# A fused attention and snake-MLP kernel: weights and values loaded in 128-partition parts, value passes by even and odd dimensions, stage orders written anew

## The chip, the cores and the metric

The kernel runs on one core of a Trainium2 chip. The metric is device time in microseconds (us), the median of several executions. Inside the core, five engines work from their own in-order queues and meet only at semaphores: TensorE (PE in the profile, its weight loads PEld), VectorE (DVE), ScalarE (ACT), GpSimd (POOL) and SyncE (SP). SP only issues transfers here; POOL issues transfers too, between its multiplications, and those are the only ones that convert float32 to bfloat16 on the way. All transfers are carried by the core's 16 DMA engines.

## What is computed

```python
def rmsnorm(x, g):
    rms = np.sqrt(np.mean(x * x, axis=-1, keepdims=True) + 1e-06)
    return x / rms * g
q_n, k_n = (rmsnorm(q, g_q), rmsnorm(k, g_k))          # 8 batches, 12 heads, 448 rows, 64 dims
scores = scale * np.matmul(q_n, k_n.transpose(0, 1, 3, 2))
attn = softmax(scores)
x = np.matmul(attn, v)                                  # then heads are joined: 3584 rows x 768
h = x @ w_in                                            # 768 x 2048
g = h + sin(alpha * h) ** 2 / (alpha + 1e-09)
out = g @ w_out                                         # 2048 x 768
```

All inputs and the output are float32.

## The kernel before

**Stages.** One stage is one batch `b` of eight. In a stage the 12 heads are taken as three chunks of four heads (`c` = 0, 1, 2; four heads are two `pp` times two `hi`). A chunk is loaded by `load_qk` (L149, buffers for three chunks), squared (token `q`, L256 on POOL or L253 on ACT), reduced (`u`, L262), turned into 1/rms (`r`, L271 and L272), the q half multiplied by both gains (`g`, L259), scaled to bfloat16 (`k`, L281), and transposed to head dimension by row: either by the DMA (`t`, L291) or by TensorE through PSUM (`p`, L304). Chunk numbers in tokens count from the stage's own batch: 0, 1, 2 are its own chunks, 3, 4, 5 the next batch's, 6 and 7 only occur in loads (`l`).

**Attention part of a stage.** `scores` (token `S`, 21 a stage: 7 key tiles for each of three chunks) runs four 64x64 matmuls (L326) and one exponential on ACT (L329). `attend` (L335) sums over keys: `o` and `v` for chunk 0 (sums of the exponentials, then values), `x` for the sums of chunks 1 and 2 together, `y` and `z` for their values. With chunks 1 and 2 a value pass handles half of the 64 dimensions, so that eight 32-column tiles fill the array: `y` takes dimensions 0 to 31, `z` 32 to 63. L364 divides and writes `xT`, the input of the MLP, with one 128-row block `kt` for each of six slices of the 768 rows. Which 32-row strip a head gets within a block is told by `strip` (L144). The rows of `w_in` have to lie in the same order, and `load_w_in` (L209) does that: two transfers of 128 partitions for chunk 0, two for chunk 1, and four of 32 partitions for chunk 2, for each half of the 2048 columns.

**The two products.** `first_product` (L384) runs 96 matmuls of 128x128 by 448 columns (L392), then the snake: sine on ACT (L370), square on POOL for even `m` (L373) and on ACT for odd `m` (L375), and L378 on DVE. `second_product` of batch `b` (L422) is cut into small steps of eight matmuls (L471) which the next stage's order puts between its scores: a digit in an order is that many steps of the current unit, `f` one of the unit after. The last batch has it at the end, whole-array (L452).

**What sets the order.** Nothing is scheduled by the compiler. `STAGE_0`, `STAGE_1` and `STAGE_N` (L32 to L58; `STAGE_N` serves batches 2 to 7) each hold a list of tokens, a list of the four PSUM bank pairs in the order in which they are taken (`bank_pair`, L132), and tasks to be done at given steps of `first_product` (key -1 to 8). Each token puts its instructions on their engines' queues in that order, so a token that waits holds up what stands behind it on the same engine. `V` loads the values of a coming batch, `W` a half of `w_in`, `O` a half of `w_out`, all from POOL; `D` is a small copy with which POOL waits for an earlier load before it issues further ones. The transfers that POOL issues share eight completion semaphores in turn, so POOL doesn't issue one before the transfer eight places earlier has landed. `blank` matmuls (L234, L322) only keep TensorE busy in the first stage.

Of the kernel before, what the change touches and what calls it, by code (L numbers as in the profile page):

```python
# [17 lines left out]
try:  # L18
# [6 lines left out]
BF16 = mybir.dt.bfloat16  # L25
# [5 lines left out]

STAGE_0 = (  # L32
    (
        "q01 L q00 u01 G u00 g0 r01 k01 q10 r00 b11 u10 q11 k00 b15 g1 u11 q20 D1 l3 p011 r1 V0 p00 u20 "
        "q21 S4 k11 S g2 S2 S3 S1 S2 k10 l4 u21 W0 r2 p1 k20 S1 S2 S1 S q31 k21 S1 D2 o1 u31 o1 q30 S2 o5 "
        "p2 S1 S1 q41 u30 v4 S q40 v3 u41 u40 W1 S S S O0 S1 S2 S y5 x7 y2 z7 r3 g3 O1 l5 r4 V1 "
    ),
    "232013331201201032132103203103210231022301230123",
    {-1: 'g4 k30 k31', 0: 'l6', 1: 'k410 k400', 2: 'k401', 3: 'D4 k411', 4: 't4', 5: 'p3 l7 q50', 6: 'q51 u50', 7: 'g5', 8: 'u51'},
)  # L40
STAGE_1 = (
    (
        "2 f f 1 f 1 S f 3 S 1 q30 S r2 2 k20 k21 1 t2 S 1 S 4 S S 2 q40 2 S o3 o2 S o1 S u30 f f l5 f o1 "
        "u40 1 f f q31 1 q41 1 u31 S 1 u41 S 3 S r3 2 g3 f f S f r4 f 1 S g4 1 k30 S V1 2 k41 2 S k40 k31 "
        "q50 v2 S g5 v5 S S t3 x4 S z5 x3 q51 y7 z2 u51 "
    ),
    "0123230231301231202021213201230132103210",
    {-1: 'l6', 0: 'l7', 2: 't4', 4: 'u50'},
)
STAGE_N = (  # L50
    (
        "r2 S 1 q40 5 f f f k20 f 1 S 3 f 1 f u40 S S f 1 k21 1 q41 q31 1 t2 S 1 V1 1 S 1 g4 1 S 2 u31 S "
        "1 u41 S 2 S f f 1 S 2 S 2 q30 S 1 S o6 o1 v4 1 v1 u30 S v1 g3 r4 v1 f f 1 k41 2 S 1 S 1 l5 1 f "
        "q50 S f k40 f S f 1 q51 t4 S 1 r3 1 k30 1 k31 S 1 x1 l6 x6 y4 y1 y2 z2 z2 z2 z1 "
    ),
    "32103020210230230310310132131313103210210",
    {-1: 'g5 t3', 0: 'u50', 5: 'u51', 6: 'l7'},
)  # L58
LAST = "0123012"

# [7 lines left out]
def kernel(  # L68
# [23 lines left out]
    nc = tc.nc  # L92
    B, H, S, D = q.shape
    D_MODEL = H * D
    D_FF = moe_w_in.shape[1]
    P = 128
    KT = D_MODEL // P
    MT = D_FF // P
    NP = H // 2
    NT = S // P  # L100
    REST = S - NT * P
    NJ = S // REST
    assert P == 2 * REST == 2 * D
    NC = NP // 2
    SCALE = float(D) ** -0.5
    HALF = D_MODEL // 2
# [7 lines left out]
    vpool = ctx.enter_context(tc.tile_pool(name="vpool", bufs=2))  # L114
# [17 lines left out]
    def bank_pair(name, dtype=F32):  # L132
        slot = int(upcoming.popleft())
        free_at.remove(slot)
        ps = psum.tile([P, 2, 2048 // mybir.dt.size(dtype)], dtype, tag=f"ps{slot}", name=name)
        slot_of[id(ps)] = slot
        return ps

    def give_back(ps):
        free_at.append(slot_of.pop(id(ps)))  # L140

    qk, vb, norm = {}, {}, {}

    def strip(c, pp, hi):  # L144

        s = 2 * hi + (pp if c == 1 else 1 - pp)
        return slice(s * 32, s * 32 + 32)

    def load_qk(ci, k_queue=nc.sync):  # L149

        b, dp = ci // NC, ci % NC
        qk[ci] = inp.tile([P, 2, 2 * NJ, D], F32, tag="qk", name="qk")
        for which, src, queue in ((0, q, nc.sync), (1, k, k_queue)):
            heads = src[b].rearrange("(dp hi pp) (p j) d -> dp (pp p) hi (j d)", hi=2, pp=2, j=NJ)[dp]
            queue.dma_start(out=qk[ci][:, which].rearrange("p (hi j) d -> p hi (j d)", hi=2), in_=heads)

    def load_v(b):


        vb[b] = vpool.tile([P, NP, NJ, D], BF16, tag="vb", name="vb")  # L160
        heads = v[b].rearrange("(g pp) (p j) d -> (pp p) g (j d)", pp=2, j=NJ)
        nc.gpsimd.dma_start(out=vb[b].rearrange("p g j d -> p g (j d)"), in_=heads)

    load_qk(0, nc.scalar)
    small = const.tile([MT, P], F32)
# [9 lines left out]
    ones = const.tile([P, D], BF16)  # L175
# [11 lines left out]
    w_in_sb = [wpool.tile([P, KT, D_FF // 2], BF16, name=f"w_in_{half}") for half in range(2)]  # L187
    w_out_sb = wpool.tile([P, MT, D_MODEL], BF16)
# [17 lines left out]
        give_back(ps)  # L206
        nc.vector.reciprocal(inv_alpha_sb, alpha_sb)

    def load_w_in(half):  # L209


        cols = slice(half * D_FF // 2, (half + 1) * D_FF // 2)
        pairs = moe_w_in.rearrange("(c hi pp d) f -> c pp hi d f", c=NC, pp=2, d=D)
        quarters = moe_w_in.rearrange("(g x d) f -> g x d f", x=2, d=D // 2)
        for pp in range(2):
            nc.gpsimd.dma_start(out=w_in_sb[half][:, pp], in_=pairs[0, pp, :, :, cols])
        for x in range(2):
            nc.gpsimd.dma_start(out=w_in_sb[half][:, 2 + x], in_=quarters[4:8, x, :, cols])
        for hi in range(2):
            for pp in range(2):  # L220
                g = 8 + 2 * hi + pp
                nc.gpsimd.dma_start(out=w_in_sb[half][strip(2, pp, hi), 4:6], in_=quarters[g, :, :, cols].rearrange("x d f -> d x f"))

    def load_w_out(half):
        src = moe_w_out.rearrange("(mt p) d -> p mt d", p=P)
        cols = slice(half * HALF, (half + 1) * HALF)
        nc.gpsimd.dma_start(out=w_out_sb[:, :, cols], in_=src[:, :, cols])  # L227

    def keep_busy(n, rhs):


        ps = bank_pair("ps")
        for _ in range(n):
            nc.tensor.matmul(ps[:, 0, :rhs.shape[-1]], blank[:, :P], rhs, start=True, stop=True)  # L234
        give_back(ps)
# [99 lines left out]
    def attend(b, what, tiles=range(NJ)):  # L335

        kind, both = what.split()
        both = both == "1"  # L340
        if tiles[0] == 0:
            avs[what] = bank_pair("av")
        av = avs[what]
        for j in tiles:
            for hi in range(2):
                for c in ((1, 2) if both else (0,)):
                    for pp in range(2):
                        r = slice(pp * 64, pp * 64 + 64)
                        o, k = (strip(c, pp, hi), c - 1) if both else (slice(hi * 64, hi * 64 + 64), pp)
                        d = slice(D // 2) if kind in ("ones", "low") and both else slice(D // 2, D) if both else slice(D)  # L350
                        w = ones[r, d] if kind == "ones" else vb[b][r, 2 * c + hi, j, d]
                        nc.tensor.matmul(av[o, k, :S], w, expT[b * NC + c, j][r, hi, :], start=(j == 0), stop=(j == NJ - 1))  # L352
        if tiles[-1] < NJ - 1:
            return
        if kind == "ones":
            rec = recs[both] = rpool.tile([P, 2, S], F32, tag="rec", name="rec")
            nc.scalar.activation(rec, av[:, :, :S], ACT.Ln)
            nc.scalar.activation(rec, rec, ACT.Exp, scale=-1.0)
            give_back(avs.pop(what))
        else:  # L360
            if b not in xT:
                xT[b] = xpool.tile([P, KT, S], BF16, tag="xT", name="xT")
            kts = slice(0, 2) if not both else slice(2, KT, 2) if kind == "low" else slice(3, KT, 2)
            nc.vector.tensor_mul(xT[b][:, kts, :], av[:, :, :S], recs[both])  # L364
            give_back(avs.pop(what))
# [135 lines left out]
    def step(b, token):  # L501

        what, n = token[0], [int(x) for x in token[1:]]
        if what == "b":
            keep_busy(int(token[1:]), blank)
        elif what == "G":
            spread_g()
        elif what == "L":
            spread_alpha()
        elif what == "W":  # L510
            load_w_in(n[0])
        elif what == "O":
            load_w_out(n[0])
        elif what == "V":
            if b + n[0] < B:
                load_v(b + n[0])
        else:
            ci = NC * b + n[0]
            if ci >= NC * B:
                return  # L520
            if what == "l":
                return load_qk(ci)
            if ci not in norm:
                norm[ci] = norm_tasks(ci)
            st = norm[ci]
            if what == "D":
                nc.gpsimd.tensor_copy(gate, qk[ci][:, 1, 0, 0:1])
            elif what == "q":
                st.square(n[1])
            elif what == "u":  # L530
                st.reduce(n[1])
            elif what == "g":
                st.fold_g()
            elif what == "r":
                st.rsqrt(slice(n[1], n[1] + 1) if n[1:] else slice(0, 2))
            elif what == "k":
                st.scale(n[1], n[2:] or (0, 1))
            elif what == "p":
                st.pe_transpose((0, 1), n[1:2] or (0, 1), act=len(n) > 2)
            elif what == "t":  # L540
                st.transpose()
            else:
                raise ValueError(token)

    UNIT = MT // 2
    for b in range(B):
# [7 lines left out]
        for x in tokens_of(plan):  # L554
# [4 lines left out]
            elif x[0] in STEPS:  # L559
                n = int(x[1:] or 1)  # L560
# [38 lines left out]
```

## Time and profile before

| | us |
|---|---|
| Device time, median of 3 | 463.21 (461.94 to 466.78) |
| Span of the profiled execution | 463.5 |
| PE busy | 413.9 (89%) |
| ACT busy | 316.3 (68%) |
| POOL busy | 275.1 (59%) |
| DVE busy | 225.8 (49%) |

Read from the start of the 96 matmuls of `first_product` in each batch, the stages lie like this (us from the start of the span):

| batch | attention part | first product |
|---|---|---|
| 0 | 0 to 37.7 | 37.7 to 72.2 |
| 1 | 72.2 to 107.4 | 107.4 to 126.5 |
| 2 | 126.5 to 162.5 | 162.5 to 180.7 |
| 3 | 180.7 to 214.4 | 214.4 to 232.7 |
| 4 | 232.7 to 264.1 | 264.1 to 282.4 |
| 5 | 282.4 to 316.9 | 316.9 to 335.2 |
| 6 | 335.2 to 367.7 | 367.7 to 386.0 |
| 7 | 386.0 to 415.7 | 415.7 to 434.0 |
| second product of batch 7 | 434.0 to 463.5 | |

A line of the waits reads: engine, line and tile that waited, what it waited for, then the total in us, the number of waits and the longest. A line of the timeline reads: start, length, engine, line, operation, tile written and read, count, and in brackets the idle time before it with what ended it. In the windows the columns after the length are the busy times of PE, PEld, DVE, ACT and POOL with instruction counts, the granted TensorE clock (1.00 is full), the busy share of the 16 DMA engines, and the rate at which bytes landed.

### The profile page before, as it was taken

The page shows a single profiled execution, that of the slowest core. Times are in us where ns is not written, and L with a number is a line of the kernel's source. Part 1 is how long each engine was busy: PE and PEld are TensorE (multiplying, and loading weights), DVE is VectorE, ACT ScalarE, POOL GpSimd, SP SyncE. Part 2 cuts the span into 40 slices and gives each one's busy share as a digit, 9 for nine tenths or more (in the row PEclk, how much of TensorE's full clock was granted, in tenths as well). Part 3 has the DMA queues.
Part 4 walks back from the last instruction along what each step waited for, and adds up shares of the span by engine and source line. Part 5 has one row for each costly group of instructions (what it writes and reads, how often), then busy time and mean ns, then how long its engine had stood idle before and what let it go on. Part 6 is the DMA issues. An engine that isn't in the chain of part 4 may idle for free.

```text
span 463.5 us, 14846 instructions
## 1 busy us (share of the span) xinstructions
PE 413.9 (89%) x6598; PEld 245.6 (53%) x6598; DVE 225.8 (49%) x331; ACT 316.3 (68%) x465; POOL 275.1 (59%) x251
## 2 busy tenths in 40 slices
PE   4988099878996999979998999979997999999796
PEld 2444046643573655655565556655574656655363
DVE  4743157433762356723765356524764365344411
ACT  4796068882896668956888778956896778976400
POOL 5945497895494945956486946856495945003200
PEclk9999689998998899989999999989999999999899
DMA  6998899799029490567419570949329510620013
GB/s 238 187 213 104 112 238 179 146 213 239 4 56 180 62 245 3 98 153 152 140 28 222 101 193 3 114 136 184 108 57 196 103 33 1 110 55 0 2 46 90
DMA packets 73188, 54.99 MB, mean 119 GB/s; under 512 B 44564, under 2 KB 68900, under 8 KB 73124
## 3 DMA queue, kind: packets, MB, share of 16 engines
q1 hardware_dynamic: 54834, 40.51, 38.6%
q0 software_dynamic: 17344, 11.83, 19.0%
q10 hardware_dynamic: 946, 1.70, 1.0%
q8 instruction: 51, 0.84, 0.8%
q14 instruction: 13, 0.11, 0.1%
HBM read 45.62 MB, written 11.01 MB: 122 GB/s over the span
## 4 chain that ended last, share of the span: by engine, by line
PE 71%; DMA 21%; POOL 3%; issue 2%; ACT 2%; DVE 1%; POOLq 0%; SPq 0%; ACTq 0%
PE hps L392 28%; PE ops L471 21%; DMA qkT<-qkn 14%; PE av L352 8%; PE sc L326 6%; PE ops L452 5%; DMA w_in<-in_moe_w_in_dram 3%; DMA qk<-in_k_dram 3%; PE ps L234 2%; DMA small<-in_moe_alpha_dram 1%; POOL qk L259 1%; POOL sq L256 1%; ACT s L370 1%; ACT expT L329 1%; POOL w_out_sb L227 1%
## 5 line engine op out<-in xcount | busy, mean ns | idle before, releaser
L329 ACT ACTIVATE expT<-sc 128x896 bf16<-128x896 f32 x168 | 142.9, 917 | 34.8 <-PE sc L326 34.4
L392 PE MATMUL hps<-xT,w_in 128*128 128x448 bf16 x768 | 149.8, 356 | 13.1 <-DVE qkn L281 12.1
L471 PE MATMUL ops<-w_out_sb,g_sb 64*64 64x384 bf16 x3072 | 154.6, 329 | 0.5 <-issue 0.5
L392 PEld LDWEIGHTS <-w_in 128*128 128x128 bf16 x768 | 74.9, 99 | 87.4 <-DVE qkn L281 12.6
L471 PEld LDWEIGHTS <-g_sb 64*64 64x64 bf16 x3072 | 99.7, 109 | 38.4 <-issue 2.1
L373 POOL TENSOR_TENSOR s<-s 128x448 f32<-128x448 f32 x64 | 59.6, 932 | 99.6 <-ACT s L370 68.3
L370 ACT ACTIVATE s<-hps,alpha_sb 128x448 f32<-128x448 f32 x128 | 74.0, 626 | 62.4 <-PE hps L392 47.2
L378 DVE SCALAR_TENSOR_TENSOR g_sb<-s,inv_alpha_sb,hps 128x448 bf16<-128x448 f32 x128 | 81.5, 677 | 63.4 <-POOL s L373 62.2
L281 POOL TENSOR_TENSOR qkn<-qk,inv 128x448 bf16<-128x448 f32 x80 | 72.8, 938 | 37.2 <-ACT inv L272 31.4
L326 PE MATMUL sc<-qkT 64*64 64x448 bf16 x672 | 68.5, 356 | 17.8 <-DMA qkT<-qkn 15.9
L256 POOL TENSOR_TENSOR sq<-qk 128x896 f32<-128x896 f32 x44 | 73.6, 1681 | 6.5 <-DMA qk<-in_k_dram 6.4
L262 DVE TENSOR_REDUCE ms<-sq 128x14 f32<-128x896 f32 x44 | 47.1, 1081 | 16.4 <-POOL sq L256 16.3
L364 DVE TENSOR_TENSOR xT<-av,rec 128x896 bf16<-128x896 f32 x24 | 25.6, 1089 | 57.0 <-PE av L352 38.9
L477 DVE COPY osb<-ops 128x384 f32<-128x384 f32 x48 | 26.7, 557 | 50.7 <-PE ops L471 50.7
L259 POOL TENSOR_TENSOR qk<-qk,gg 128x896 f32<-128x896 f32 x24 | 50.1, 2089 | 2.1 <-ACT gg L198 1.5
L352 PE MATMUL av<-expT,vb 64*32 64x448 bf16 (+1 forms) x1120 | 41.8, 358 | 4.6 <-issue 4.6
L326 PEld LDWEIGHTS <-qkT 64*64 64x64 bf16 x672 | 24.9, 107 | 34.7 <-DMA qkT<-qkn 18.3
L375 ACT ACTIVATE s<-s 128x448 f32<-128x448 f32 x64 | 36.9, 577 | 3.1 <-DVE g_sb L378 0.8
L352 PEld LDWEIGHTS <-vb 64*32 64x32 bf16 (+1 forms) x1120 | 21.1, 97 | 16.5 <-issue 7.2
L478 DVE TENSOR_TENSOR osb<-osb,ops 128x384 f32<-128x384 f32 x48 | 26.6, 554 | 1.7
L352 PE MATMUL av<-expT,ones 64*32 64x448 bf16 (+1 forms) x672 | 25.3, 350 | 0.0
L452 PE MATMUL ops<-w_out_sb,g_sb 128*128 128x384 bf16 x128 | 22.4, 341 | 3.1 <-DVE g_sb L378 3.1
(48 smaller groups left out, 167.4 us busy)
## 6 DMA issues: line engine op xcount, KB each, us to landing
qk<-in_q_dram SPq DMA_DIRECT2D x24, 448.0 KB, 5.6
qk<-in_k_dram SPq DMA_DIRECT2D x22, 448.0 KB, 6.1
out_dram<-osb SPq DMA_DIRECT2D x39, 192.0 KB, 3.0
vb<-in_v_dram POOLq DMA_DIRECT2D x8, 672.0 KB, 9.8
w_out_sb<-in_moe_w_out_dram POOLq DMA_DIRECT2D x2, 1536.0 KB, 20.1
out_dram<-osb SPq DMA_DIRECT2D x26, 96.0 KB, 3.0
w_in<-in_moe_w_in_dram POOLq DMA_DIRECT2D x8, 256.0 KB, 16.7
w_in<-in_moe_w_in_dram POOLq DMA_DIRECT2D x8, 128.0 KB, 16.6
```

Source lines behind the costliest of these rows:

```text
L256: nc.gpsimd.tensor_mul(st.sq[w], qk[ci][:, w], qk[ci][:, w])
L259: eng.tensor_mul(qk[ci][:, 0], qk[ci][:, 0], gg.to_broadcast([P, 2 * NJ, D]))
L262: nc.vector.reduce_sum(st.ms[:, w, :], st.sq[w], axis=AX.X)
L281: eng.tensor_mul(n[:, :, hi, :], x[:, hi], inv[:, hi].unsqueeze(2).to_broadcast([P, NJ, D]))
L326: nc.tensor.matmul(sc[pp * 64:pp * 64 + 64, hi, :S], qkt[r, 1, j * REST:(j + 1) * REST], qkt[r, 0, :], start=True, stop=True)
L329: nc.scalar.activation(expT[c, j], sc[:, :, :S], ACT.Exp, scale=SCALE)
L352: nc.tensor.matmul(av[o, k, :S], w, expT[b * NC + c, j][r, hi, :], start=(j == 0), stop=(j == NJ - 1))
L370: nc.scalar.activation(s1, hps, ACT.Sin, scale=alpha_sb[:, m, :])
L373: nc.gpsimd.tensor_mul(s2, s1, s1)
L378: nc.vector.scalar_tensor_tensor(g_sb[:, m, (b % 2) * S:(b % 2 + 1) * S], s2, inv_alpha_sb[:, m, :], hps, op0=ALU.mult, op1=ALU.add)
L392: nc.tensor.matmul(ps[:, m % 2, :S], w_in_sb[m * 2 // MT][:, kt, m % (MT // 2) * P:(m % (MT // 2) + 1) * P], x[:, kt, :], start=(kt == ORD ...
L471: nc.tensor.matmul(st["ps"][os, r, :HALF], g_sb[rs, m, c0 + o * 64:c0 + o * 64 + 64], w_out_sb[rs, m, half * HALF:(half + 1) * HALF], star ...
```

## The change

- `w_in` comes in by half and chunk (`load_w_in(half, c)`). For chunks 1 and 2 one transfer brings 256 rows to 128 partitions, partition `p` taking rows `2p` and `2p + 1`. No 32-partition transfers are left: four transfers a half in place of eight.
- That puts even rows into one block and odd rows into the next, so the value passes `y` and `z` take the even and the odd dimensions, with weights read at a step of two.
- In chunk 2 the two heads of a pair sit the other way round in the strips. So that the strips are right, chunk 2's q, k and v are loaded with the two 64-partition halves exchanged: two transfers of 64 partitions in place of one of 128.
- `v` comes by chunk (`load_v(b, c)`: one, one and two transfers, in place of one for all), and each half of `w_out` in two parts.
- All three orders, bank lists and task lists are new. Batch 1's third chunk is squared already in the first stage, and batch 1's second and third chunks are transposed by TensorE (56 more transposing matmuls, 36 DMA transposes in place of 40), and in `STAGE_N` the loads of `v` stand ahead of the scaling of chunk 2 and in the first product, no longer right behind its transposes.

The transfers are meant to use the DMA engines better and to bring what is needed first, and the orders are meant to fit them.

```diff
@@ STAGE_N (tokens; tasks beside the first product) @@
-        "r2 S 1 q40 5 f f f k20 f 1 S 3 f 1 f u40 S S f 1 k21 1 q41 q31 1 t2 S 1 V1 1 S 1 g4 1 S 2 u31 S "
-        "1 u41 S 2 S f f 1 S 2 S 2 q30 S 1 S o6 o1 v4 1 v1 u30 S v1 g3 r4 v1 f f 1 k41 2 S 1 S 1 l5 1 f "
-        "q50 S f k40 f S f 1 q51 t4 S 1 r3 1 k30 1 k31 S 1 x1 l6 x6 y4 y1 y2 z2 z2 z2 z1 "
+        "1 r2 q31 q30 f 2 S V10 f 3 V11 f f 2 S k20 3 S 2 k21 S u31 q40 1 t2 2 S 1 f u30 g3 S 2 f S f S "
+        "r3 q41 f f 1 l5 1 f S 3 u40 1 S S 5 S S u41 o7 v7 S S 5 S 2 q51 k31 f S 2 S q50 k30 2 S g4 1 u50 "
+        "S 2 r4 t3 1 S z3 x7 k40 y7 z1 z2 z1 "
...
-    {-1: 'g5 t3', 0: 'u50', 5: 'u51', 6: 'l7'},
+    {-1: 'l6 u51 V12', 1: 'k41', 2: 't4 l7', 3: 'g5'},
@@ STAGE_0 (tokens from the first W on; tasks) @@
-        "... W0 r2 p1 k20 S1 S2 S1 S q31 k21 S1 D2 o1 u31 o1 q30 S2 o5 "
-        "p2 S1 S1 q41 u30 v4 S q40 v3 u41 u40 W1 S S S O0 S1 S2 S y5 x7 y2 z7 r3 g3 O1 l5 r4 V1 "
+        "... V00 q11 u11 p00 q10 V02 W11 p011 S4 u10 q20 r1 "
+        "g1 S4 q21 S1 l3 u20 S1 k11 k10 S4 u21 S g2 r2 p1 k20 S2 V01 S2 S o3 q30 W00 S W12 k21 l4 o4 D2 "
+        "q40 W01 p2 l5 S1 g4 S u30 q31 W02 g3 u40 v1 q41 S v6 u31 S W10 S S3 S1 S3 x2 S S x1 S1 u41 x2 y2 "
+        "q51 y3 x2 z1 z1 y2 z1 z1 q50 r4 r3 z2 z1 O00 k31 "
...
+    {-1: 'u50 k30 u51 O01', 1: 'k401 O10', 2: 'k410 k411', 3: 'O11', 4: 'V10', 5: 'k400', 6: 'D4 l6 V11', 7: 'p3', 8: 'V12 g5 l7 p4'},
@@ load_qk @@
+            if dp < 2:
+                queue.dma_start(out=rows, in_=heads.rearrange("pp p hi x -> (pp p) hi x"))
+            else:
+                for pp in range(2):
+                    queue.dma_start(out=rows[pp * 64:pp * 64 + 64], in_=heads[1 - pp])
@@ load_w_in(half, c) @@
-        for x in range(2):
-            nc.gpsimd.dma_start(out=w_in_sb[half][:, 2 + x], in_=quarters[4:8, x, :, cols])
-        for hi in range(2):
-            for pp in range(2):
-                g = 8 + 2 * hi + pp
-                nc.gpsimd.dma_start(out=w_in_sb[half][strip(2, pp, hi), 4:6], in_=quarters[g, :, :, cols].rearrange("x d f -> d x f"))
+        rows = moe_w_in[c * 2 * P:(c + 1) * 2 * P, cols]
+        if c:
+            nc.gpsimd.dma_start(out=w_in_sb[half][:, 2 * c:2 * c + 2], in_=rows.rearrange("(p x) f -> p x f", x=2))
@@ attend @@
-                        d = slice(D // 2) if kind in ("ones", "low") and both else slice(D // 2, D) if both else slice(D)
+                        d = slice(kind == "high", D, 2) if both and kind != "ones" else slice(D // 2 if both else D)
```

In the tokens of the new version `W` takes half and chunk (`W11` is the second half of the columns, chunk 1), `O` half and part, `V` batch offset and chunk.

## The prediction

> **What bounds the kernel now.** I read the table of engines first: PE is busy for 413.9 of 463.5 us, so at most 49.6 us can be had without less PE work, and the question is where PE stands still. The waits tell it. A line gives who waited for what, total, times, longest:
>
> ```profile
> PE sc L326 <- DMA qkT<-qkn: 15.9, 6, 4.3
> PE hps L392 <- DVE qkn L281: 12.1, 1, 12.1
> POOL w_out_sb L227 <- DMA w_in<-in_moe_w_in_dram: 9.8, 1, 9.8
> PE av L352 <- issue: 4.6, 3, 3.9
> ```
>
> There are two stories: one stop of 12.1 us in the first product of batch 0, and one wait for DMA transposes in six stages. The timeline of POOL shows what led to the first:
>
> ```profile
> 36.27 0.87 POOL L216 DMA_DIRECT2D w_in<-in_moe_w_in_dram  x1
> 38.41 0.81 POOL L216 DMA_DIRECT2D w_in<-in_moe_w_in_dram  x1 [1.26 <-DMA w_in<-in_moe_w_in_dram]
> ...
> 40.54 2.14 POOL L222 DMA_DIRECT2D w_in<-in_moe_w_in_dram  x4
> 52.51 1.19 POOL L227 DMA_DIRECT2D w_out_sb<-in_moe_w_out_dram  x1 [9.83 <-DMA w_in<-in_moe_w_in_dram]
> ```
>
> The second half of w_in is issued only at 36.27, its first part lands at 52.2, and POOL can't issue w_out before (its semaphore is that part's). Behind L227 stand the gain (L259) for which DVE waits at L281, and the snake's squares (L373), so ACT and PE stop. By the windows the DMA engines were meanwhile not full:
>
> ```profile
> 37.00:42.00 5.00, 4.10 (x54) 1.88 (x33) 2.54 (x3) 2.91 (x7) 3.74 (x7) 1.00 0.59 56
> 52.00:55.00 3.00, 0.00 (x0) 0.00 (x0) 0.00 (x0) 0.00 (x0) 2.47 (x2) 0.50 0.49 53
> 68.00:72.00 4.00, 4.00 (x23) 2.01 (x21) 3.74 (x7) 2.95 (x5) 3.76 (x4) 1.00 1.31 203
> ```
>
> The last columns are clock, DMA share and GB/s: 53 to 56 GB/s while w_in crawls, 203 with w_out alone. The second story, in the timeline of batch 4 (SP and PE):
>
> ```profile
> 242.18 4.11 SPq L291 DMA_TRANSPOSE qkT<-qkn  x2
> 243.28 0.88 POOL L162 DMA_DIRECT2D vb<-in_v_dram  x1
> 251.92 0.38 PE L326 MATMUL sc<-qkT 64*64 64x448 bf16 x2 [1.35 <-DMA qkT<-qkn]
> ```
>
> The transposes of chunk 2 (token t2) are issued at 242.18, a whole batch of v (672 KB) joins them 1.1 us later, and the second lands at 251.9, 9.7 us after the start; the median of all 40 is 4.8 us from issue to landing. In batch 2 the same takes 12.6 us and PE stands for 4.30.
>
> **What the Trainium skill says.** "SBUF — State Buffer", section "Door 1: The DMA port swizzle", says that 32 partitions, and also partitions 0 to 63, reach 8 of the 16 ports, and gives 189 and 196 GB/s for these against 328 for 128 partitions at 1 MiB. The trace agrees in direction: the slow windows fall in the time of the 32-partition parts (L222); it doesn't separate them from other causes. The same section says that a step in SBUF is free as long as at least two accesses fall into a line of 16 bytes; at a step of two, bfloat16 has four. No run of before has such a weight load. "DMA: Bandwidth & Descriptors", section "Issuing engines are not separate DMA queues", says that transfers of POOL and SP interleave on the same 16 engines; the trace agrees (9.7 us with v beside, 4.8 median). Its table "Rules for kernel authors" says that two transfers to the two partition halves serialize; before has none.
>
> **The change part by part.**
>
> 1. *Head, attention of batch 0.* PE runs its first scores at 15.9, after blank matmuls that stay 26. From there ACT is the limit (21.99 busy of 22.7 us to 37.7). The new order has the same 21 exponentials, so I leave 37.7 and add 0.5.
>
> 2. *Head, first product.* POOL now issues W11 before chunk 2's squares and the other w_in parts between squares. I add up its queue from row durations, with D1 behind one gain (7.54 + 2.08 = 9.6): V00, V02 (two), W11 at about 0.65 each reach 12.3; q20 1.68, g1 2.08, q21 1.68, g2 2.08 reach 19.9; V01, q30, W00 (2 x 0.84), W12, q40 reach 27; W01, g4, q31, W02 reach 32; g3, q41, W10 (1.7) reach 37.4; q51 and q50 (3.4) and O00 reach 41.6, O01 42.3. So all of w_in is issued by 37.4 where the old order ended at 42.7, and its last part is 0.5 MB landed, 2.6 us at the 203 GB/s of w_out, with some 2 us of start: near 42. It is needed when m = 8 begins, 9.1 us after the start (half of 18.3), at 47. No semaphore comes late: each of these transfers waits for one issued at least eight places earlier (O00 for V01). Up to here the stop of 12.1 and the smaller waits for w_in vanish. The product then costs what it costs in batches 2 to 7, 18.3, plus two transposes p3 and p4 of 0.89 each (the row of L304 with 28 matmuls), and I leave 1.5 for parts that land late or squares that stand behind an O or V issue. End: 38.2 + 18.3 + 1.8 + 1.5 = 59.8, against 72.2. **Gain 12.4.**
>    Can the DMA do it? By then chunks 0 to 6 (7 x 0.92 MB, at 337 to 345 GB/s in windows that hold only q and k: 19 us), w_in, w_out and two v (7.7 MB landed at 203: 38 us) must pass: 57 of the 57 us from 3 to 60. It fits because half of w_out and v are needed later still (v at 16.9 us into the next stage).
>
> 3. *Batch 1.* Attention now takes 35.2 us. Its work: batch 7, with nothing loaded and nothing waited for, has 29.4 us of PE for 56 steps; batch 1 has 48, so 29.4 - 8 x 0.325 (a step is 8 matmuls, 0.65 for 16) = 26.8, plus p2 by PE, 0.9: 27.7. I leave 1.5. The product goes from 19.1 to 18.3. The wait for t2 is gone, since p2 takes its place; its 1.2 us of DVE copies lie beside 29 us with DVE half idle. Part of the old loss is the 3.9 us that PE stood with "issue" as the only reason; I count it as gone, which may be wrong. **Gain 6.0 + 0.8 = 6.8.**
>
> 4. *Batches 2 to 6.* The attention parts take 36.0, 33.7, 31.4, 34.5 and 32.5, together 168.1; batch 7's 29.7 five times is 148.5, so 19.6 is excess. It is the wait for t2 plus the slow clock after it (37 steps' matmuls took 2.93 us after the 4.3 us wait, 1.49 after the 1.35 us wait). New order: POOL is free 1.7 us into the stage (its last square), then q31, q30 (3.4), V10, V11 (1.4, taken from the 0.69 of L218), k20, k21 (4 x 0.93): t2 can go at 10.2, against 9.5 now. Two thirds of v (2.3 us of DMA at 203 GB/s) go ahead of it, the last third has moved into the first product. Landing: 10.2 + 1.4 + 4.8 = 16.4. PE reaches score 15, which needs it, after 40 steps, 14 scores and 14 units of o and v: 40 x 0.325 + 28 x 0.19 = 18.3; the same sum for the old order gives 17.6 where the trace has 17.5. So there are 1.9 us to spare where 1.4 to 4.3 were missing. What is added: three more v issues a stage on POOL (4 x 0.65 - 0.88 = 1.7 us, POOL is busy 35 of 50), two SP issues of 0.5 (SP waits far longer than that), and l5 as half-partition loads right behind t2. From the port figures I estimate 4.7 us for l5 where 2.7 would do; q51 on POOL waits for it, till about 22, and k31, q50, k30, g4, k40 behind it end near 32, just before the first square of the product at 34. I leave 1.2 a stage. **Gain 19.6 - 6.0 = 13.6.**
>
> 5. *Strided weights, batch 7, the tail.* y and z: taken as free. From below zero; from above the loads (93 ns, 896 of them) could double. They are overlapped by four row and column groups, and a pass of 56 takes 1.5 to 1.7 us. Doubling y and z wholly would cost 8 x 3.3 = 26 us. I take zero for the four accesses per line. Batch 7 and the last 29.5 us have no edit that touches their bound: zero.
>
> Sum: 463.2 - 12.4 - 6.8 - 13.6 = 430.4.
>
> **The rivals.**
> A. *A new wait takes the old one's place in the stages*: l5 and the stores behind t2, or q51 holding POOL's queue, cost 3 to 4 us a stage. For it: POOL's queue has 2 us of slack by my sum, l5 now rides on half the ports. Against it: DMA share in these stages is about 0.6. Time: head in full, half of batch 1, nothing in 2 to 6: 463.2 - 12.4 - 3.4 = 447.4.
> B. *The head is bound by the volume of loads*: 57 of 57 us leaves nothing. First product ends near 69: 463.2 - 3 - 6.8 - 13.6 = 439.8. Against it: only w_in must have come by 47.
> C. *Slower*: strided loads cost 2.3 times the passes, 1.3 x 26 = 34 us more: 464.4, and anything on top of it is slower by over 1%. For it only that the trace has no such load.
>
> **How the numbers follow.** Forecast 0.62, A 0.18, B 0.13, C 0.07. Time: 430.4. The lower end is all leftovers gone, 14.4 - 0.5 + 8.3 + 19.6 = 41.8 less, 421.4; the upper end takes in B and most of A: 449. Outside it are C and the worst of A. Faster by over 1% (below 458.6) is the first three, 0.93; within 1% 0.02; slower 0.05.
>
> **What would show it.** Step 2: PE L392 in batch 0 without an idle line over 2 us, w_out issued near 42, batch 1 starting near 60. Step 3: attention of batch 1 near 29. Step 4: no PE wait for qkT over 1 us, attention parts of 30 to 31. Step 5: y and z passes of 1.5 to 1.7 us. A wait for qk or qkT in each stage makes A right, a wait for w_in or w_out before 75 us makes B right.

## The result, and the profile after

| | before | changed |
|---|---|---|
| Device time, median (us) | 462.57 (461.87 to 466.78) | 430.74 (429.09 to 431.65) |
| Ratio, with 95% interval | | 0.929 (0.923 to 0.935) |
| Span of the profiled execution | 463.5 | 429.9 |
| PE busy | 413.9 (89%) | 408.5 (95%) |
| Mean granted TensorE clock | 0.967 | 0.988 |

The forecast was 430.4 us. The sum is right to 0.3 us, but the terms are not: one part of it came out 8.1 us worse, and four others made that good. So the closeness of the total is luck. The stages show it (us in the one profiled execution, which was the longest of the four, so the differences don't add up to the 0.3; "attention" runs to the first matmul of the next first product):

| part | forecast | measured | difference |
|---|---|---|---|
| start to batch 1 (attention of 0, first product, p3, p4) | 59.8 | 67.9 | +8.1 |
| attention of batch 1 | 29.2 | 27.9 | -1.3 |
| attention of batches 2 to 6 | 148.5 + 6.0 = 154.5 | 29.2 + 30.3 + 32.7 + 29.5 + 29.9 = 151.6 | -2.9 |
| attention of batch 7 | 29.7 | 29.0 | -0.7 |
| last second product | 29.5 | 25.0 | -4.5 |

The first products of batches 1 to 7 take 18.3 to 18.5 us each, as forecast.

The waits of the changed kernel answer to the four lines shown of before (engine, line and tile; what was waited for; total us, times, longest):

```profile
POOL sq L264 <- DMA qk<-in_k_dram: 27.6, 7, 6.3
PE hps L400 <- DMA w_in<-in_moe_w_in_dram: 6.0, 4, 4.7
PE av L360 <- DVE osb L486: 4.3, 4, 2.1
```

The wait for `qkT` (15.9 us) and the stop of 12.1 us are gone. In their place PE waits for `w_in` and, a little, for DVE. POOL's wait for k has grown from 6.4 us and is now the longest of these in total. What ended the head is in the timeline of POOL (start, length, engine, line, operation, tile):

```profile
22.64 1.67 POOL L230 DMA_DIRECT2D w_in<-in_moe_w_in_dram  x2
24.30 0.74 POOL L227 DMA_DIRECT2D w_in<-in_moe_w_in_dram  x1
...
27.43 0.77 POOL L227 DMA_DIRECT2D w_in<-in_moe_w_in_dram  x1
31.89 0.75 POOL L227 DMA_DIRECT2D w_in<-in_moe_w_in_dram  x1
36.32 1.69 POOL L230 DMA_DIRECT2D w_in<-in_moe_w_in_dram  x2
...
41.79 1.86 POOL L235 DMA_DIRECT2D w_out_sb<-in_moe_w_out_dram  x2
```

and in that of PE:

```profile
39.37 0.36 PE L400 MATMUL hps<-xT,w_in 128*128 128x448 bf16 x1 [0.21 <-DMA w_in<-in_moe_w_in_dram]
40.08 1.50 PE L400 MATMUL hps<-xT,w_in 128*128 128x448 bf16 x7 [0.35 <-DMA w_in<-in_moe_w_in_dram]
46.23 1.68 PE L400 MATMUL hps<-xT,w_in 128*128 128x448 bf16 x4 [4.65 <-DMA w_in<-in_moe_w_in_dram]
48.72 17.77 PE L400 MATMUL hps<-xT,w_in 128*128 128x448 bf16 x84 [0.82 <-DMA w_in<-in_moe_w_in_dram]
```

L230 loads chunk 0 of `w_in`, L227 chunks 1 and 2. POOL nearly kept the forecast schedule: all of `w_in` is issued by 38.0 (37.4 forecast), the first column half of `w_out` by 43.7 (42.3 forecast). The landing did not keep it:

```profile
DMA to landing us min/median/max: 8.6/16.6/18.8
```

The first four tiles `m` of the product go block by block, so they need the whole first half of `w_in` at once. PE waits for its chunk 0 (issued from 22.64), for its chunk 1 (issued at 27.43, 4.65 us of waiting) and for its chunk 2. The chain of waits (start, length, what) has the transfer on it that releases the last line above:

```profile
31.89 16.79 DMA w_in<-in_moe_w_in_dram
48.72 17.77 PE hps L400 x84
```

Issued at 31.89, it lands at 48.7. The windows say what the DMA engines did meanwhile (after the length: PE, PEld, DVE, ACT, POOL busy; clock, DMA share, GB/s landed):

```profile
42.00:47.00 5.00, 0.77 (x3) 0.33 (x4) 3.65 (x6) 0.14 (x1) 1.66 (x2) 0.84 0.75 107
47.00:52.00 5.00, 4.18 (x12) 1.45 (x11) 0.00 (x0) 0.00 (x0) 0.00 (x0) 0.50 1.18 261
```

107 GB/s while PE stands, 261 in the 5 us after: the engines moved far less than they could when PE needed the bytes. The second line also shows the aftermath: the clock is at 0.50, and the 96 matmuls take 21.3 us of work where 18.3 is usual.

The stage of batch 4, in the timelines of SP, POOL, DVE and PE in that order (one line of each):

```profile
220.38 2.66 SPq L299 DMA_TRANSPOSE qkT<-qkn  x2
...
231.96 1.68 POOL L264 TENSOR_TENSOR sq<-qk 128x896 f32<-128x896 f32 x1 [6.28 <-DMA qk<-in_k_dram]
...
237.10 1.09 DVE L270 TENSOR_REDUCE ms<-sq 128x14 f32<-128x896 f32 x1 [3.71 <-POOL sq L264]
...
239.29 3.73 PE L360 MATMUL av<-expT,vb 64*32 64x448 bf16 x88 [2.06 <-DVE osb L486]
```

The transposes go out 10.1 us into the stage (210.28 to 220.38; 10.2 forecast) and PE never waits for them. But POOL waits 6.28 us for a k that was loaded behind them, DVE's sum of squares waits for POOL, and the copies of the output that stand behind it on DVE come late for PE. This is the longest stage, 32.7 us. Part of that belongs to this one execution: in experiments 1 and 2, which leave these loads and orders as they are, the same stage takes 30.0, 33.2 and 30.2 us.

### The profile page after: what moved, and what is told of

Same layout as the page of the kernel before. It is cut to its first block, busy times and chain, and to the rows that moved or that the text cites. A ratio compares the mean times of both kernels' runs of the same rounds, so it can differ in the third digit from the quotient of the medians.

```text
span 429.9 us, 14999 instructions
## 1 busy us (share of the span) xinstructions
PE 408.5 (95%) x6657; PEld 239.5 (56%) x6657; DVE 227.5 (53%) x335; ACT 316.8 (74%) x465; POOL 285.9 (67%) x269
## 2 busy tenths in 40 slices
DMA packets 68485, 54.08 MB, mean 126 GB/s; under 512 B 39860, under 2 KB 64196, under 8 KB 68420
## 4 chain that ended last, share of the span: by engine, by line
PE 84%; DMA 6%; POOL 3%; DVE 2%; ACT 2%; issue 1%; POOLq 0%; SPq 0%
PE hps L400 34%; PE ops L479 27%; PE av L360 10%; PE sc L334 6%; PE ops L460 5%; DMA w_in<-in_moe_w_in_dram 4%; POOL sq L264 2%; PE ps L242 2%; ACT expT L337 2%; DMA qk<-in_q_dram 1%; DMA small<-in_moe_alpha_dram 1%; POOL qkn L289 1%; PE tp L312 1%; DVE ms L270 1%; DVE osb L486 1%
## 5 line engine op out<-in xcount | busy, mean ns | idle before, releaser
L337 ACT ACTIVATE expT<-sc 128x896 bf16<-128x896 f32 x168 | 144.6, 918 | 15.6 <-PE sc L334 14.9
L479 PE MATMUL ops<-w_out_sb,g_sb 64*64 64x384 bf16 x3072 | 146.1, 323 | 0.0
L378 ACT ACTIVATE s<-hps,alpha_sb 128x448 f32<-128x448 f32 x128 | 74.5, 626 | 54.1 <-PE hps L400 50.3
L381 POOL TENSOR_TENSOR s<-s 128x448 f32<-128x448 f32 x64 | 59.4, 932 | 82.3 <-ACT s L378 59.3
L479 PEld LDWEIGHTS <-g_sb 64*64 64x64 bf16 x3072 | 89.8, 107 | 39.3 <-issue 2.2
L264 POOL TENSOR_TENSOR sq<-qk 128x896 f32<-128x896 f32 x44 | 73.6, 1678 | 28.3 <-DMA qk<-in_k_dram 27.6
L334 PE MATMUL sc<-qkT 64*64 64x448 bf16 x672 | 56.9, 351 | 0.4 <-DVE qkT L319 0.2
L270 DVE TENSOR_REDUCE ms<-sq 128x14 f32<-128x896 f32 x44 | 47.0, 1079 | 16.8 <-POOL sq L264 16.8
L360 PE MATMUL av<-expT,vb 64*32 64x448 bf16 (+1 forms) x1120 | 38.1, 362 | 4.3 <-DVE osb L486 4.3
L372 DVE TENSOR_TENSOR xT<-av,rec 128x896 bf16<-128x896 f32 x24 | 25.5, 1088 | 30.2 <-ACT rec L366 24.0
L360 PEld LDWEIGHTS <-vb 64*32 64x32 bf16 (+1 forms) x1120 | 19.2, 97 | 19.1 <-DVE osb L486 6.4
L334 PEld LDWEIGHTS <-qkT 64*64 64x64 bf16 x672 | 20.2, 106 | 13.3 <-issue 4.5
L486 DVE TENSOR_TENSOR osb<-osb,ops 128x384 f32<-128x384 f32 x48 | 26.6, 554 | 1.7
L460 PE MATMUL ops<-w_out_sb,g_sb 128*128 128x384 bf16 x128 | 21.0, 326 | 0.0
```

The costliest lines, as they stand in the source:

```text
L264: nc.gpsimd.tensor_mul(st.sq[w], qk[ci][:, w], qk[ci][:, w])
L270: nc.vector.reduce_sum(st.ms[:, w, :], st.sq[w], axis=AX.X)
L334: nc.tensor.matmul(sc[pp * 64:pp * 64 + 64, hi, :S], qkt[r, 1, j * REST:(j + 1) * REST], qkt[r, 0, :], start=True, stop=True)
L337: nc.scalar.activation(expT[c, j], sc[:, :, :S], ACT.Exp, scale=SCALE)
L378: nc.scalar.activation(s1, hps, ACT.Sin, scale=alpha_sb[:, m, :])
L381: nc.gpsimd.tensor_mul(s2, s1, s1)
```

## The experiments

Each ratio is to the kernel before, run in the same series: its median was 466.5 us beside experiments 1, 4, 5 and 6, 466.2 beside 3, 7, 8 and 10, and 465.3 beside 2 and 9, against 462.6 beside the changed kernel. The changed kernel itself was not run again in these series, so a difference of two or three us from its 430.7 is uncertain by the times alone; there the stages of the traces have to decide.

**1. Chunk 0 of w_in in four transfers.** In the changed kernel, each transfer of L230 is cut in two:

```diff
-nc.gpsimd.dma_start(out=w_in_sb[half][:, pp], in_=rows.rearrange("(hi pp d) f -> pp hi d f", hi=2, pp=2)[pp])
+for hi in range(2):
+    g = 2 * hi + pp
+    nc.gpsimd.dma_start(out=w_in_sb[half][hi * 64:hi * 64 + 64, pp], in_=rows[g * D:(g + 1) * D])
```

> The changed kernel, with w_in's chunk 0 (the parts W00 and W10) loaded as four transfers of 64 rows each in place of two of 128 rows whose DRAM side has the two heads as its slowest dimension. Same bytes, same places. Theory 1: these two transfers run on few DMA engines each and hold up what is queued behind them on those engines, so that W02, issued at 31.9, lands at 48.7. Then PE's waits for w_in (6.0 us in all, longest 4.65) fall below 1 us, batch 1 starts at 61 to 62 in place of 67.9, and the time falls by 5 to 7 us, to 424 to 426. Theory 2: the DMA engines are full with the volume, or with the half-partition loads of q and k. Then the waits stay at 5 to 7 us and the time at 430 to 431.

Measured: 420.93 us (420.26 to 422.6), ratio 0.905 (0.899 to 0.910). The median from issue to landing of all `w_in` transfers falls from 16.6 to 5.9 us, the wait of PE from 6.0 to 0.2, and the first product of batch 0 ends at 57.7 instead of 66.5. The window in which PE stood, now:

```profile
42.00:47.00 5.00, 5.00 (x29) 2.56 (x27) 3.59 (x6) 2.64 (x6) 4.99 (x6) 1.00 0.33 36
```

The DMA engines have little left to do (36 GB/s), because the bytes came earlier. So the way in which chunk 0 is cut cost the changed kernel about 9.8 us, more than I had expected, since the slow clock after the stop goes too: 8.8 us of it are the earlier end of the first product.

**2. Which property of the cut?** The four-part version changes two things: the outermost step of the source, which counts 2 (`hi`) before and 64 rows after, and the number of transfers under way. Two kernels separate them. The first keeps two transfers a half but cuts them by `hi`, so that the outermost step counts 64 (each then writes 64 partitions instead of 128):

```diff
-for pp in range(2):
-    nc.gpsimd.dma_start(out=w_in_sb[half][:, pp], in_=rows.rearrange("(hi pp d) f -> pp hi d f", hi=2, pp=2)[pp])
+for hi in range(2):
+    nc.gpsimd.dma_start(out=w_in_sb[half][hi * 64:hi * 64 + 64, 0:2], in_=rows[hi * P:hi * P + P].rearrange("(pp d) f -> d pp f", pp=2))
```

> The changed kernel with chunk 0 of w_in still in two transfers a half, as many and as large as in the changed kernel, but cut by partition halves, so that the outermost step of the source counts 64 rows instead of 2. Theory 1 (the outermost count of the source sets how many DMA engines carry a transfer): as fast as the four-part version, 420 to 423 us, w_in landing near 6 us in the median, no PE wait for w_in above 0.5 us, and some 3500 packets fewer on the POOL queue than the changed kernel's 16096. Theory 2 (what mattered was having four smaller transfers under way instead of two): no change, 428 to 432 us, landing near 16 us.

The second makes four transfers of half the columns each and leaves the outermost step at 2:

```diff
 for pp in range(2):
-    nc.gpsimd.dma_start(out=w_in_sb[half][:, pp], in_=rows.rearrange(...)[pp])
+    for f in range(2):
+        cut = slice(f * D_FF // 4, (f + 1) * D_FF // 4)
+        nc.gpsimd.dma_start(out=w_in_sb[half][:, pp, cut], in_=rows[:, cut].rearrange(...)[pp])
```

> The changed kernel with chunk 0 of w_in in four transfers a half, each half as large, but cut by columns, so that the outermost step of the source still counts 2. Theory 1 (outermost count sets the number of engines): no gain, 428 to 435 us, w_in landing 14 us or more in the median, a PE wait for w_in of 3 us or more stays, and the packets don't fall below 16096. Theory 2 (number of transfers under way): 420 to 424 us as in the four-part version cut by partitions.

Measured: cut by `hi` 420.59 us (420.19 to 425.32), ratio 0.903 (0.898 to 0.907), landing 7.6 us in the median, no PE wait for `w_in`. Cut by columns 428.01 us (426.82 to 433.44), ratio 0.918 (0.913 to 0.923), landing 11.6 us, and this in its waits:

```profile
PE hps L401 <- DMA w_in<-in_moe_w_in_dram: 5.2, 2, 3.4
```

So turning the cut round, with as many transfers as before, brings the whole gain, and doubling their number with a 2 left outermost brings little: the first product of batch 0 ends at 65.5 instead of 66.5, against 57.7 when cut by `hi`. The rest of the 2.7 us to 430.7 lies in batch 4, whose length varies. The landing is not the 14 us or more that I had expected. "DMA: Bandwidth & Descriptors" of the Trainium skill, section "Why a DMA increments its semaphore by 16 and not by 1", has the rule: a transfer is spread over the largest number of engines up to 16 that divides the outermost count of both of its sides. Here that is 2 of 16 for chunk 0. No record names the engines, but the packets of the POOL queue fit. The profile counts, for the changed kernel, for the cut by `hi` and for the cut by columns (packets, MB, share of 16 engines):

```profile
q0 software_dynamic: 16096, 11.82, 19.0%
```

```profile
q0 software_dynamic: 12512, 11.81, 18.8%
```

```profile
q0 software_dynamic: 20256, 11.84, 20.0%
```

The bytes are the same. Cutting the four transfers that have a 2 outermost by `hi` removes 3584 packets, which is 4 x 896, and 896 is 14 engines by 64. Over all queues the packets under 512 B are 39860 and 36276 in the two kernels, again 3584 apart, so the packets that went were all small ones. Four more transfers with a 2 outermost add 4160, or 4 x (896 + 144). That is what one would see if each engine without a share got 64 packets with next to nothing in them per transfer; the count is shown, the meaning is inferred. The full 128-partition transfers of L227 were slow because they shared the queue with those of L230: with L230 alone altered, their median falls from 17.5 to 9.9 us (9.7 in experiment 1).

**3. The old kernel with only this cut.** Each of its chunk-0 transfers (L216) is cut in two by `hi`:

```diff
-nc.gpsimd.dma_start(out=w_in_sb[half][:, pp], in_=pairs[0, pp, :, :, cols])
+for hi in range(2):
+    nc.gpsimd.dma_start(out=w_in_sb[half][hi * 64:hi * 64 + 64, pp], in_=pairs[0, pp, hi, :, cols])
```

> The kernel before, with w_in's chunk 0 loaded as four transfers of 64 rows a half in place of two of 128 rows whose DRAM side has the two heads as its slowest dimension; chunks 1 and 2 as they were, in transfers of four heads by 32 rows and in 32-partition strips. Theory 1 (few engines): the chunk 0 transfers also held up the old kernel. POOL's wait ahead of w_out falls from 9.8 to 1 to 5 us, PE's stop of 12.1 us to 3 to 8, batch 1 starts at 64 to 69 in place of 72.2, time 455 to 460. Theory 2 (the 32-partition strips and their ports are the cause, as forecast): the stop stays at 10 to 12 us and the time within 2 us of before.

Measured: 459.13 us (454.63 to 461.3), ratio 0.985 (0.978 to 0.992). The first product of batch 0 shrinks from 34.5 to 24.5 us and batch 1 starts at 62.7. POOL's wait ahead of `w_out` falls from 9.8 to 0.3 us and PE's stop of 12.1 to 2.5. But only 7.0 us arrive at the end: the stages still wait for their transposes (18.4 us in all, 15.9 before), and the last second product is 1.4 us longer at a lower clock. The head isn't free of slow parts either: the old chunk 1 has four heads outermost, and its parts of 0.25 MB still land after 9.2 to 15.8 us, where those of chunk 0, now half as large, land after 4.6 to 7.0.

**4. New orders on the old transfers.** The changed kernel with the old parts of `w_in`, the values in halves, whole loads of q, k and v and no exchange of heads (edits: the old bodies of `load_w_in` and of the slice at L358, `< 3` for `< 2` in the loads).

> The changed kernel with its new orders, but with the old layout: w_in's chunk 1 in two transfers and chunk 2 in four of 32 partitions, value passes by halves of the dimensions, no exchange of heads, so q, k and v of chunk 2 in whole 128-partition transfers. Theory 1 (the old w_in parts are slow on few engines or ports): PE's waits for w_in rise from 6.0 to 10 to 16 us, batch 1 starts at 72 to 78; the stages themselves gain up to 1 us each from whole loads; time 432 to 438. Rival (the new orders alone bring the gain, the layout nothing): waits for w_in within 1 us of 6.0, time 426 to 431. In both, if strided weights cost nothing, the passes y and z of 56 matmuls keep their 1.5 to 1.7 us.

Measured: 436.31 us (434.88 to 436.78), ratio 0.937 (0.931 to 0.942). The orders, with `v` by chunk and `w_out` in parts, bring most of the gain. The head is worse than with the new parts (the first product of batch 0 ends at 77.7 instead of 66.5), the stages better: 29.0 to 29.2 us in all of batches 2 to 7. PE waits 8.4 us for `w_in`, less than the 10 us or more that I had expected, but 6.1 more for DVE's `xT`: POOL stands 7.5 us before it can issue the old chunk 2, its squares come late, and DVE, which waits for them, writes `xT` late. Experiment 5 differs from this one only in the parts of `w_in` and the step of the weights and is 8.4 us faster. So much the new parts of `w_in` are worth under these orders; whether by the 4 outermost in the old chunk 1 or by the smaller number of issues was not separated. Value passes cost the same: `av` matmuls are at 350 ns here with contiguous weights, and at 350 in experiment 1 with weights at a step of two.

**5. The exchange of heads.** The changed kernel with q, k and v of chunk 2 loaded whole. This leaves the exchange out: chunk 2's heads then meet each other's rows of `w_in`, so it serves for its times alone.

```diff
-            if dp < 2:      # load_qk; likewise c in load_v
+            if dp < 3:
```

> The changed kernel with q, k and v of chunk 2 in whole transfers of 128 partitions. The exchange of the two heads of a pair is thereby left out, so the heads of chunk 2 meet each other's rows of w_in. Theory: the half-partition loads are what makes the third chunk of the next batch late (POOL L264 waits 27.6 us for k in seven waits, longest 6.3), DVE stands behind that square, and PE then waits 4.3 us for DVE at L486. Then POOL's wait falls to 10 to 16 us, PE's wait for L486 below 1.5 us, and the time by 3 to 6 us, to 425 to 428. Rival: the transfers are issued late in SP's queue and the halves cost nothing: waits within 15%, time 429.5 to 431.

Measured: 427.89 us (426.66 to 429.05), ratio 0.919 (0.913 to 0.925). POOL's wait for k falls from 27.6 to 22.2 us, less than expected, but its longest is now 4.4 and PE no longer feels it (wait for L486 0.2 us, 4.3 in the changed kernel); batches 2 to 7 take 29.0 to 29.4. In the profiled executions these six stages gain 5.4 us together, while the first product of batch 0 ends 2.1 us later. The halves cost about 2.8 us by the times of the two kernels, and experiment 10, which cuts chunk 2 of `w_in` anew besides, is 2.0 us faster than experiment 1.

**6. v behind the transposes again, in the changed kernel.** Old place of v, all else new:

```diff
-r2 q31 q30 f 2 S V10 f 3 V11 f f 2 S k20 ... q40 1 t2 2 S ...    {-1: 'l6 u51 V12', ...}
+r2 q31 q30 f 2 S f 3 f f 2 S k20 ... q40 1 t2 V10 V11 V12 2 S ...  {-1: 'l6 u51', ...}
```

> The changed kernel with all loads of v in batches 2 to 7 moved to right behind the DMA transposes of chunk 2 (token t2), where the old order had them; nothing else moved. Theory: v beside the transposes is what made them land late. Then PE waits for qkT again, 1 to 4 us in each of batches 2 to 6, and the time rises by 4 to 14 us, to 435 to 445. Rival: the old wait came from where the transposes stood in the order, and the new order has enough room: waits for qkT under 1 us, time 430 to 432.

Measured: 443.13 us (441.14 to 445.7), ratio 0.952 (0.944 to 0.960). The time is as expected, the way is not. No PE wait for `qkT` came back: the transposes land after 7.5 us at most, and the new order has room for that. Instead the waits read:

```profile
POOL sq L264 <- DMA qk<-in_k_dram: 28.8, 6, 5.9
PE av L360 <- DVE osb L486: 11.3, 5, 2.9
```

POOL, held by the v issues and then by a late k (its half loads land after 7.8 us in the median, 4.9 in the changed kernel), holds DVE (24.9 us of waiting for L264, 16.8 in the changed kernel), and DVE holds PE for 11.3 us where it was 4.3. Batches 2 to 6 take 30.8 to 33.6 us.

**7. v before the transposes, in the old kernel.** One token is moved:

```diff
-r2 S 1 q40 5 f f f k20 ... t2 S 1 V1 1 S 1 g4
+r2 S 1 q40 V1 5 f f f k20 ... t2 S 1 1 S 1 g4
```

> The kernel before, with the load of v in batches 2 to 7 moved ahead of the scaling of chunk 2 (behind q40) from its place right behind the DMA transposes of chunk 2. Nothing else. Theory: v beside the transposes made them late. Then PE's waits for qkT fall from 15.9 us to 1 to 4 us, the attention parts of batches 2 to 6 from 33.6 on the mean to 30 to 31, and the time by 10 to 17 us, to 447 to 454. Rival: the transposes land late for their own place in the order (they go out no earlier, and are needed at 17.5 us into the stage), v is beside the point: waits over 10 us, time 459 to 465.

Measured: 441.01 us (439.82 to 442.11), ratio 0.947 (0.940 to 0.953), more than expected. The waits have this left of 15.9 us:

```profile
PE sc L326 <- DMA qkT<-qkn: 0.6, 1, 0.6
```

Batches 2 to 7 take 29.0 to 29.6 us. The two transposes land 6.8 us after the first is issued in batch 2 and 5.6 in batch 4, where the old kernel had 12.6 and 9.7. So the second story of the prediction holds in the old kernel: what made the transposes late was v beside them. The attention parts of batches 2 to 6 fall by 21.8 us together. PE's idle time is 14.9 of it; the other 6.9 are busy time for the same matmuls, at granted clocks of 0.91 to 1.00 before and 1.00 now, which is the slow clock after the waits. The few us that are left lie in batch 1 and in the tail and were not traced to a cause.

**8. The last second product.** In the old kernel, the bank pairs of the last batch in another order:

```diff
-LAST = "0123012"
+LAST = "3210321"
```

> The kernel before, with the bank list of the last second product begun at bank pair 3 in place of 0 (LAST 3210321 for 0123012). Nothing else. Bank pair 0 holds the last tile of the first product until DVE has written its g, bank pair 3 has long been free. Theory: the 3.1 us that PE waits for DVE (L378) ahead of the last 128 matmuls, and the slow clock after it, come from the bank alone: then the tail from the last first product to the end falls from 29.5 to 25 us and the time by 4 to 5 us, to 458 to 460. Rival: the matmuls wait for the g values themselves, or the clock was slow for another reason: tail 28.5 to 29.5, time unchanged within 1 us.

Measured: 458.74 us (455.57 to 462.3), ratio 0.985 (0.979 to 0.992). The old kernel's timeline of PE begins the last product like this:

```profile
437.04 3.27 PE L452 MATMUL ops<-w_out_sb,g_sb 128*128 128x384 bf16 x10 [3.09 <-DVE g_sb L378]
```

With another pair first there is no such wait, and the tail takes 24.8 us instead of 29.5. That is 4.7 us, where the medians are 7.4 apart; the profiled execution shows no other gain, and where the rest comes from is open. The same line of the changed kernel:

```profile
404.72 20.96 PE L460 MATMUL ops<-w_out_sb,g_sb 128*128 128x384 bf16 x128
```

All 128 matmuls in one piece, right behind the last matmul of the first product. `LAST` is the same in both kernels and begins with pair 0; the list of `STAGE_N` ended with pair 0 before and ends with pair 3 now, so the new bank lists did this.

**9. Three small edits in the old kernel.** Experiments 3, 7 and 8 together, and nothing else of the change.

> The kernel before with three small edits together: the loads of v moved ahead of the scaling of chunk 2, the last second product beginning with the bank pair that is free, chunk 0 of w_in in four transfers a half. Theory 1 (the three add up: 25.2 for v, 7.7 for the banks of which 2 to 3 belong to other stages, 7.0 to 10 for the head): 466.2 less 35 to 42, 424 to 431 us; no wait for qkT, batch 1 starting near 63, attention parts of 29 to 30, tail near 25. Rival (what the head gains is given back in the stages, as when it was done alone): 433 to 440 us with attention parts over 31.

Measured: 430.42 us (428.49 to 431.94), ratio 0.924 (0.919 to 0.929). That is the time of the whole change (0.929, 0.923 to 0.935). Batch 1 starts at 64.0, batches 2 to 7 take 29.0 to 29.8 us, the tail 24.8. It is at the slow end of what adding up gave; attention of batch 1 stays at 33.8 us (35.2 in the old kernel), where the change has 27.9. PE's timeline in that part has these lines:

```profile
77.36 1.17 PE L472 MATMUL ops<-w_out_sb,g_sb 64*64 64x384 bf16 x24 [2.13 <-DMA w_out_sb<-in_moe_w_out_dram]
80.61 1.66 PE L472 MATMUL ops<-w_out_sb,g_sb 64*64 64x384 bf16 x36 [1.72 <-issue]
97.21 0.75 PE L353 MATMUL av<-expT,vb 64*32 64x448 bf16 x21 [2.25 <-issue]
```

**10. A version that beats both.** The cut of experiment 1, and the exchange of heads moved out of the loads of q, k and v (whole again) into the rows of `w_in`, whose chunk 2 comes in four parts of 32 partitions:

```diff
+if c == 2:
+    for hi in range(2):
+        for pp in range(2):
+            g = 2 * hi + pp
+            nc.gpsimd.dma_start(out=w_in_sb[half][strip(2, pp, hi), 4:6], in_=rows[g * D:(g + 1) * D].rearrange("(p x) f -> p x f", x=2))
```

> The changed kernel, with w_in's chunk 0 in four transfers of 64 rows; and with the exchange of heads in chunk 2 moved from the loads of q, k and v, which become whole 128-partition transfers, to w_in, whose chunk 2 comes in four strips of 32 partitions. Theory: strips of 32 partitions are harmless when they run on all engines, and whole loads of q and k end the lateness of the third chunk. Then waits for w_in stay under 1.5 us, PE's wait for L486 falls from 4.3 to under 1.5 us, and the time to 416 to 419, 2 to 5 us under the kernel with chunk 0 split alone (420.9). Rival: the strips bring back the wait for w_in (3 us or more), and the time is 421 to 426.

Measured: 418.89 us (418.55 to 419.2), ratio 0.900 (0.895 to 0.905). No wait for `w_in` is listed, none of PE for DVE's copies of the output, and batches 2 to 7 take 29.0 to 29.3 us. All `w_in` transfers together have a median of 6.2 us to landing, and the 32-partition parts among them take 6.0 to 8.1.

## Why the prediction was right, and where it wasn't

The total was right, and so was the mechanism in the stages. In the head the landing of `w_in` was wrong, and the tail was left out; these two terms missed by more than my leftovers, in opposite directions, and that they cancel is luck.

*Step 1.* The first product starts at 39.4, where 38.2 was said. What the extra 1.2 us are was not tried.

*Step 2, the head, is where it failed.* The term is "its last part is 0.5 MB landed, 2.6 us at the 203 GB/s of w_out, with some 2 us of start: near 42". The issues of `w_in` held to 0.6 us, but I took a rate from `w_out`, whose transfers have 128 rows outermost, for `w_in`, whose chunk 0 has a 2 there. That last part landed at 53.6, 16.4 us after its issue, where I had 4.6. It was also the wrong part to ask about: PE never waited for it. I dated only what the second half of the tiles needs; PE waited for the first half of `w_in`, which landed at 39.3 to 48.7, 16.5 to 18.8 us after its issues. At 4.6 us a part it would have been there by 36.5. From 59.8: start of the product +1.2, PE's waits inside it +5.8, slow clock after them +3.0, leftover not needed -1.5, transposes 1.4 instead of 1.8: -0.4. That is 67.9. The result looks like rival B (near 69), yet volume was not the cause: with another cut and the same bytes the product ends at 57.7, and at 59.3 with p3 and p4, against my 59.8. The port swizzle, which I named beside the slow windows of before, is not supported either: 64-partition parts (5.9 and 7.6 us in the median, experiments 1 and 2) and 32-partition parts (6.0 to 8.1, experiment 10) land fast.

*Step 3.* Batch 1 took 27.9 us; the 1.5 us that I left were hardly used, and the 3.9 us of "issue" did vanish with the new order. Experiment 9, with the old order, keeps such pauses. Why they arise stays open.

*Step 4.* The excess over batch 7 was 19.6 us, 6.0 were left for the new order, 3.1 came. The mechanism stands on experiment 7. Experiment 6 adds a correction: in the new order v beside the transposes does harm through POOL and DVE, and not through `qkT`. Rival A was right in kind: k behind the transposes does hold POOL's queue, through DVE it reached PE, and experiment 5 shows that the half-partition loads are what makes it felt. Its size was 2 to 3 us in the whole kernel, not 3 to 4 a stage.

*Step 5.* The strided weights are free: 350 ns a matmul with and without. This agrees with what "SBUF — State Buffer" of the Trainium skill, section "Door 1: The DMA port swizzle", states: a step costs nothing while at least two accesses fall into a line of 16 bytes. But "batch 7 and the last 29.5 us have no edit that touches their bound: zero" was wrong by 4.5 us. I read the new bank lists as a matter of the stages and never looked at what the first matmul of the tail waited for; the trace of before shows it (3.09 us for L378, the line in experiment 8), and the matmuls after it ran at a lower clock.

So 8.1 us lost in the head are balanced, by luck and not by the argument, by 1.3 + 2.9 + 0.7 + 4.5 = 9.4 elsewhere. With chunk 0 cut otherwise, the same change takes 421 us, at the low end of my range.

## What to carry to other kernels

Before taking a rate from one transfer for another, look at the outermost count of each side of its access pattern: a rearranged source with a 2 outside made 0.25 MB crawl and held up the well-formed transfers behind it, and turning the cut round, with as many transfers, was worth about 10 us of 431. When a wait of PE is removed, count its slow clock too; in batches 2 to 6 of the old kernel 14.9 us of standing still came with 6.9 us of slower matmuls (experiment 7). And look for the small edit inside the large one: a token, a string of bank numbers and one cut of a transfer, 430.4 us together, equal the whole rewrite as it was made.

## What the runs showed of the hardware that I had not expected

- Two transfers of 0.25 MB with a 2 as the outermost count, a queue of full ones behind them: 16.6 us from issue to landing in the median of all `w_in` transfers, against 7.6 when as many transfers of the same size have 64 outermost (experiment 2). Each such transfer goes with 896 packets more on the queue, while the bytes stay.
- A stop of PE of 4.65 us is followed by a clock of 0.50 in the window from 47 to 52 us; it cost 3.0 us more of matmul time.
- A batch of v issued right behind two transposes made them land after 9.7 us in batch 4 and 12.6 in batch 2 of the old kernel, counted from the first one's issue to the second one's landing, but after 8.9 us at most in experiment 6, as far as the trace shows the landings, where it comes in four parts. Moved ahead of them, 5.6 and 6.8 (experiment 7). Whether the parts or their time of issue make the difference was not tried.
